# Weighted sums as 64-row, 32-column tiles in two of 32 units of an attention kernel

## The chip, the cores and the metric

The kernel runs on one core of a Trainium2 chip. The metric is the device time of one execution in microseconds (us). A core has five engines that work side by side: TensorE (PE, matrix products; its weight loads are listed apart as PEld), VectorE (DVE), ScalarE (ACT), GpSimd (POOL), and SyncE (SP), which here only issues DMAs. Each takes its instructions in the order in which the program lists them. TensorE's products land in PSUM banks of 128 partitions by 512 fp32 values; DVE and ACT read them there.

## What is computed

The reference mixes two attentions over the same 2048 positions of width 512, with 32 heads of 16 values each. Branch A looks back over 8 positions, 2 apart. Branch B is full attention with one shared key and value head. A gate per position mixes them.

```python
def _B_ref(x, wq, wk, wv, wo):
    q = (x @ wq).reshape(B, S, H, Dh).transpose(0, 2, 1, 3)
    k = x @ wk
    v = x @ wv
    scores = einsum("bhqd,bkd->bhqk", q, k) * (Dh ** -0.5)
    p = softmax(scores, axis=-1)
    o = einsum("bhqk,bkd->bhqd", p, v)
    return o.transpose(0, 2, 1, 3).reshape(B, S, H * Dh) @ wo

g = sigmoid((x * gate_w).sum(-1, keepdims=True))
return g * _A_ref(...) + (1 - g) * _B_ref(...)
```

The change concerns `o` of branch B: the sum over the keys of softmax weight times value.

## The kernel before

Branch B is cut into 32 **units**: 4 blocks of 512 queries by 8 groups of 4 heads. A unit takes 16 **steps**, one for each block of 128 keys, so the main loop (L1272) runs over 512 steps `s`, with `u, kt = divmod(s, 16)`.

A step does the following on its engines.

- `exp_pair` (L577), called twice: two score products on PE (L582), each of 64 rows (one half of the array for each of two heads), into the two halves of one double bank (`eb[0]` or `eb[1]`), and then one exponential on ACT over both (L584), which gives a tile `pexp`. A double bank is written again only after ACT has read it.
- `weighted` (L589), for the step before: the four heads' `pexp` tiles are multiplied with the block's values `vst`, which have 16 value columns and 16 columns of ones. The matmul of head `i` contracts all 128 keys and writes 32 partitions of the bank `po`. The four outputs together fill `po`, which gathers the sums over the unit's 16 steps. These are fp32 products, and each shows in the profile as two rows, while the scores are of a type that shows one row.
- Maxima for later units. The softmax needs each query's largest score before its unit begins, so the scores are formed once more with the queries as rows (L393) and reduced by DVE. `fill_pair` forms two into the double bank `m2` (named `pm` in the profile; reduced at L422), usually once a step. `fill_one` forms one, a **single**, into the bank `m1` (named `ps`; L433), where `singles` (L986) allows it.

After the last step of a unit, `finish_a` (L604) transposes `po` on DVE into `tt`. `finish_b` takes the reciprocal of the sums on DVE and scales on POOL. The next unit's weighted sums write `po` again, so they wait for the transpose.

The order of all instructions is fixed as the program is written out: a planner keeps a clock for each engine (`clk`) and a time at which each bank comes free (`free`), advanced by `after` with assumed durations, and decides by them what is issued where. `fill_ready` (L1011) issues a pair or a single only if its bank is expected to be free in time. `single_share` (L995) sets the rate of singles: the maxima still to go, less two for each step left (the pairs) and less an allowance for the output phases, divided by the steps left, at most one a step. `singles` spends that share. No single is asked for in a unit's first step until the last units.

Twice, at about 824 us and 1166 us, an output phase (`out_phase`, L864) stands between two units. It multiplies finished rows with the output weights and forms maxima beside them in another way (L491). Branch A's attention runs on POOL through the first two thirds of the span, and its projections on PE before the first unit.

Of the kernel before, what the change touches and what calls it, by code (L numbers as in the profile page):

```python
# [6 lines left out]
F32 = mybir.dt.float32  # L7
F32R = mybir.dt.float32r
AF = mybir.ActivationFunctionType
# [4 lines left out]
P = 128  # L14
# [4 lines left out]
NJ = S // P  # L19
# [26 lines left out]
M2H = 0.15  # L46
JUST = 0.05
WB = 6


T_R, T_LAT, T_EXP, T_RED2, T_RED1, T_W, T_TTR = 0.23, 0.20, 0.92, 1.14, 0.61, 1.21, 0.66
# [30 lines left out]
def gated_mix_kernel(ctx, tc, xt, wa, wk, wq, wo_a, wo_b, out):  # L82
    nc = tc.nc
# [11 lines left out]
    vst = cp.tile([P, NJ, 32], F32, name="vst")  # L95
# [14 lines left out]
    m1 = pp.tile([P, 512], F32, name="ps")  # L110
    po = pp.tile([P, 512], F32, name="po")
# [5 lines left out]
    def split(hi, lo, src, eng=None):  # L117
        high(hi, src)
        (eng or nc.vector).tensor_sub(lo, src, hi.bitcast(F32))

    clk = {"pe": 0.0, "act": 0.0, "dve": 0.0}

    def after(eng, ready, dur):
        clk[eng] = max(clk[eng], ready) + dur
        return clk[eng]
# [17 lines left out]
    raw = [first[:, k, :] for k in range(4)]  # L143
    raw += [p1.tile([P, 512], F32, name="xraw", tag=tag, bufs=WB) for tag in ("wah", "wal") for _ in range(6)]
    xraw = {(t, c): raw[C * t + c] for t in range(NQB) for c in range(C)}
# [15 lines left out]
    def load_wa(gg, c):  # L161
        waraw[gg, c] = p1.tile([P, GN], F32, name="waraw", bufs=2)
        nc.gpsimd.dma_start(waraw[gg, c], wa[c * P:(c + 1) * P, gg * GN:(gg + 1) * GN])

    def split_wa(gg, c):
        nonlocal pool
        wah[gg, c] = p1.tile([P, GN], F32R, name="wah", bufs=WB)
        wal[gg, c] = p1.tile([P, GN], F32R, name="wal", bufs=WB)
        split(wah[gg, c], wal[gg, c], waraw.pop((gg, c)), nc.gpsimd)
        after("act", clk["pe"], 0.62)  # L170
        pool = max(pool, clk["pe"] * 1e3) + 1300

    def ahead_wa(gg, k):

        if 0 <= k < 2 * C and k % 2 == 0:
            load_wa(gg, k // 2)
        if 2 < k <= (2 * C if gg == 0 else 2 * (WB - C)) + 1 and k % 2:
            split_wa(gg, (k - 3) // 2)
# [193 lines left out]
    free = {"m2": 0.0, "m1": 0.0, "e0": 0.0, "e1": 0.0, "po": 0.0}  # L372
# [22 lines left out]
    def to_go():  # L395
        return 2 * len(slots) + len(half)
# [178 lines left out]
    pe, pexp, exped = [], {}, {}  # L575
# [12 lines left out]

    def weighted(s):  # L589
        u, kt = divmod(s, NJ)  # L590
        for i in (3, 2, 1, 0):
            nc.tensor.matmul(po[32 * i:32 * i + 32, :], vst[:, kt, :], pexp[s, i // 2][:, i % 2, :], start=(kt == 0), stop=(kt == NJ - 1))  # L592
        del pexp[s, 0], pexp[s, 1]
        after("pe", exped.pop(s) + 0.1, T_W)

# [7 lines left out]

    def finish_a(u, eng):  # L604
        tt = pe[0].tile([P, 4 * 4, 32], F32, name="tt", bufs=2)
        nc.vector.transpose(tt.rearrange("p b d -> p (b d)"), po)
        at = after("dve", clk["pe"] + T_LAT, 0.7)
        tasks.append((clk["pe"] + 0.5, finish_b, (u, tt, eng)))

# [375 lines left out]

    def singles(s):  # L986

        most = to_go() - 2 * max(0, 16 * (NU - 1) - 16 - s) - PER_ROW * max(0, NJ - 4 - outs)
        need = -0.6 if s > NJ and s % NJ == 1 else 0.3 if bare[0] else 0.5 if (s + 1) % NJ == 0 else 1.0
        if most <= 0 or share[0] < need or not bare[0] and s % NJ != 1 and share[0] < 2.0 and clk["dve"] - clk["pe"] > BEHIND:  # L990
            return False
        share[0] -= 1.0
        return True
# [228 lines left out]
    def done_mm(at):  # L1222
        nonlocal pool
        x, i = at
        lump = lumps[x]
        if lump[0] == "a" and lump[2] == NJ - 1 and lump[1] + 1 < GG and i in (2, 5) and WB - C < 4:
            c = WB - C + (i == 5)
            if c < C:
# [43 lines left out]
    for s in range(NS + 1):  # L1272
        u, kt = divmod(s, NJ)
# [16 lines left out]
        rows = 4 if outs else 8  # L1290
# [23 lines left out]
        while order:  # L1314
            which = order.pop(0)
            if which == "later":
                order[:0] = ["m1", 1] if free["e1"] > clk["pe"] - E1S or bare[0] and free["m1"] < clk["pe"] - 1.0 else [1, "m1"]
                first = 0
            elif which == "m2":
                fill_ready("m2", M2S)  # L1320
            elif which == "m1":
                one = not later_rows and (kt or not s or u >= NU - 8) and singles(s)
                bare[0] = not one
                if one:
                    first = half[0][4] if half else 0
                    fill_ready("m1", M1S)
            elif s < NS:
                if which == 1:
                    spread_some(some)
                exp_pair(s, which % 2 or which // 2, which == 2, first)  # L1330
        if s == NS:
            spread_some(some)
        if s:
            weighted(s - 1)
            if kt == 0 and s < NS:
                finish_a(u - 1, nc.gpsimd)
# [14 lines left out]
    tt = pe[0].tile([P, 16, 32], F32, name="ttl", tag="tt", bufs=2)  # L1351
# [4 lines left out]
    both = pe[0].tile([P, 2, 256], F32, name="own2", tag="tt", bufs=2)  # L1356
# [61 lines left out]
```

## Time and profile before

| | us |
|---|---|
| median of 3 runs | 1452.81 (1452.70 to 1452.86) |
| span of the profiled execution (first to last instruction) | 1450.8 |
| PE busy | 1443.6 |
| ACT busy | 1284.9 |
| DVE busy | 1192.2 |
| POOL busy | 994.6 |

The profile page is from one execution, recorded by the hardware. It has each engine's busy time, and a chain of work that ended last: from the last instruction back, at each step, to what released it. Its views list instructions in groups (by line, engine and shape, with their count and mean length) or in order of time; in brackets stands the idle time of the engine ahead of an instruction and what ended it. "128*32 128x512" at a matmul means 128 rows and 32 columns of the array, and 128 x 512 values that stream through. Matmuls overlap, and their ends are modelled, so the distance from start to start says more than a length.

Most of the span is the 512 steps. Units 10 and 12 lie at about 590 to 624 us and 657 to 691 us, between the end of the front part (about 260 us) and the first output phase.

### The profile page before, as it was taken

To read this page: it belongs to the slowest core of one execution; us is meant where nothing else is said; L and a number is where in the kernel's file an instruction comes from. 1 tells how busy PE (TensorE), PEld (TensorE's weight loads), DVE (VectorE), ACT (ScalarE), POOL (GpSimd) and SP (SyncE) were. 2 spreads that over 40 slices of the span, in tenths; PEclk is the share of its full clock that TensorE was granted. 3 is DMA by queue.
4 is the path that set the end of the run, shared out by engine and by line. 5 is a ranking of instruction groups with operands and counts; after the bars stand their busy time and mean duration, and the time that the engine had idled before them with its cause. 6 is when DMAs were issued, how large, how long until landed. Compare 5 with 4: busy or idle time off the path is not lost.

```text
span 1450.8 us, 29082 instructions
## 1 busy us (share of the span) xinstructions
PE 1443.6 (100%) x10620; PEld 678.7 (47%) x10620; DVE 1192.2 (82%) x1867; ACT 1284.9 (89%) x1628; POOL 994.6 (69%) x1748
## 2 busy tenths in 40 slices
PE   9999999999999999999999999999999999999998
PEld 7977777433333333333333476333333364333343
DVE  8978889688888888888888888888888888888712
ACT  6659888999999999999999888999999988999986
POOL 7952989869898888888988899797888240011121
PEclk9999999999999999999999999999999999999999
DMA  7753433212021120211211202021120000000110
GB/s 238 221 157 103 125 104 97 64 57 87 14 85 42 46 90 13 72 42 42 83 42 42 72 24 98 12 72 42 42 72 12 12 27 16 13 2 1 29 32 29
DMA packets 75775, 89.80 MB, mean 62 GB/s; under 512 B 56880, under 2 KB 56928, under 8 KB 71408
## 3 DMA queue, kind: packets, MB, share of 16 engines
q1 hardware_dynamic: 68544, 48.74, 11.9%
q0 software_dynamic: 6368, 37.90, 7.8%
q8 instruction: 83, 1.36, 0.4%
q10 hardware_dynamic: 720, 1.31, 0.3%
q14 instruction: 60, 0.49, 0.1%
HBM read 60.03 MB, written 27.35 MB: 60 GB/s over the span
## 4 chain that ended last, share of the span: by engine, by line
PE 99%; DVE 1%; ACT 0%; issue 0%; POOL 0%; DVEq 0%; POOLq 0%; ACTq 0%
PE po L592 35%; PE pe L582 24%; PE pe L1219 12%; PE pm L393 8%; PE ps L393 6%; PE pe L876 4%; PE pm L491 3%; PE ps L491 2%; PE po L491 2%; PE pm L947 1%; PE pe L227 1%; PE po L193 0%; PE po L393 0%; PE pm L1219 0%; PE po L1046 0%
## 5 line engine op out<-in xcount | busy, mean ns | idle before, releaser
L584 ACT ACTIVATE pexp<-pe 128x1024 f32<-128x1024 f32 x1022 | 987.1, 1022 | 80.3 <-PE pe L582 76.8
L422 DVE TENSOR_REDUCE mx<-pm 128x2 f32<-128x1024 f32 x507 | 620.1, 1223 | 140.6 <-PE pm L393 136.8
L592 PE MATMUL po<-pexp,vst 128*32 128x512 f32 x4096 | 545.5, 605 | 0.0
L582 PE MATMUL pe<-qst,kst 64*128 64x512 f32 x1916 | 443.9, 451 | 0.0
L582 PEld LDWEIGHTS pe<-qst,kst 64*128 64x128 f32 x1916 | 179.9, 183 | 473.4 <-ACT pexp L584 466.2
L433 DVE TENSOR_REDUCE mx<-ps 128x1 f32<-128x512 f32 x400 | 272.1, 680 | 0.5 <-PE ps L393 0.5
L393 PE MATMUL pm<-kst,qst 62*128 62x512 f32 x978 | 198.1, 397 | 0.4 <-ACT pexp L584 0.4
L656 POOL TENSOR_TENSOR pr<-aext 128x256 f32<-128x256 f32 x256 | 182.1, 738 | 3.0 <-DMA aext<-ad 2.8
L716 POOL TENSOR_TENSOR oa<-oa,av 128x256 f32<-128x256 f32 x224 | 164.0, 732 | 15.1
L592 PEld LDWEIGHTS po<-pexp,vst 128*32 128x32 f32 x4096 | 80.5, 108 | 163.8 <-issue 155.1
L393 PE MATMUL ps<-kst,qst 62*128 62x512 f32 x392 | 154.3, 394 | 0.0
L713 POOL TENSOR_TENSOR av<-aext,lg 128x256 f32<-128x256 f32 x224 | 139.3, 622 | 13.3
L520 ACT ACTIVATE dd<-pm 128x512 f32<-128x512 f32 x180 | 101.5, 606 | 16.4 <-PE pm L491 8.0
L1219 PE MATMUL pe<-wah,xl 64*128 64x512 f32 x376 | 110.0, 394 | 0.0
L1219 PE MATMUL pe<-wal,xh 64*128 64x512 f32 x376 | 108.6, 394 | 0.0
L1219 PE MATMUL pe<-wah,xh 64*128 64x512 f32 x376 | 107.7, 395 | 0.4 <-DVE stage L324 0.3
L393 PEld LDWEIGHTS pm<-kst,qst 62*128 62x128 f32 x978 | 95.4, 186 | 3.6 <-ACT pexp L584 0.9
L662 POOL TENSOR_TENSOR tr<-pr 128x512 f32<-128x512 f32 x64 | 81.8, 1278 | 4.5
L520 ACT ACTIVATE pexp<-pm 128x512 f32<-128x512 f32 x124 | 70.1, 606 | 14.1 <-PE pm L491 7.0
L662 POOL TENSOR_TENSOR tr<-tr 128x256 f32<-128x256 f32 (+1 forms) x128 | 72.4, 566 | 8.5
L619 POOL TENSOR_TENSOR rl<-rl,gate_t 128x16 f32<-128x16 f32 x31 | 6.9, 222 | 103.0 <-DVE rl L613 95.3
L393 PEld LDWEIGHTS ps<-kst,qst 62*128 62x128 f32 x392 | 73.2, 187 | 3.7 <-issue 1.2
(226 smaller groups left out, 1993.9 us busy)
## 6 DMA issues: line engine op xcount, KB each, us to landing
aext<-ad POOLq DMA_DIRECT2D x32, 1056.0 KB, 5.5
qst<-qd SPq DMA_DIRECT2D x60, 128.0 KB
ad<-stage SPq DMA_DIRECT2D x32, 240.0 KB
qd<-qhi SPq DMA_DIRECT2D x16, 256.0 KB
qd<-qlo SPq DMA_DIRECT2D x16, 256.0 KB
xraw<-xt SPq DMA_DIRECT2D x15, 256.0 KB
qst<-qd SPq DMA_DIRECT2D x60, 64.0 KB
qst<-ml SPq DMA_DIRECT2D x216, 2.0 KB
```

The lines of the kernel that those rows point to most:

```text
L393: nc.tensor.matmul(dst, qst[home(v)[0]][b:b + 62, pr, t * P:(t + 1) * P], kst[b:b + 62, kc * 512:(kc + 1) * 512], start=True, stop=True)
L422: nc.vector.tensor_reduce(m[:, :, pr, t, kc], dst, AX.X, ALU.max)
L433: nc.vector.tensor_reduce(m[:, odd, pr, t, kc:kc + 1], dst, AX.X, ALU.max)
L520: nc.scalar.activation(d[:, odd], m2[:, odd, :], AF.Abs)
L582: nc.tensor.matmul(bank[:, odd, :], kst[b:b + 64, kt * P:(kt + 1) * P], qst[home(u)[0]][b:b + 64, pr, :], start=True, stop=True)
L584: nc.scalar.activation(e, bank, AF.Exp, scale=SCALE)
L592: nc.tensor.matmul(po[32 * i:32 * i + 32, :], vst[:, kt, :], pexp[s, i // 2][:, i % 2, :], start=(kt == 0), stop=(kt == NJ - 1))
L656: nc.gpsimd.tensor_mul(pr[:, k], q, e[:, o:o + NH, AC:2 * AC])
L662: nc.gpsimd.tensor_add(nx, cur[:, :, 0:n], cur[:, :, n:2 * n])
L713: nc.gpsimd.tensor_mul(av, e[:, o:o + NH, 2 * AC:].rearrange("p j (h d) -> p j h d", d=DH), lg[:, w].unsqueeze(3).to_broadcast([P, NH, AG, ...
L716: nc.gpsimd.tensor_add(ao, ao, av)
L1219: nc.tensor.matmul(front[2 if x == last else x % 2][0][:, b, :], l[h], r[h], start=(i == 0), stop=(i == 3 * C - 1))
```

## The change

In units 10 and 12 each product of the weighted sum is cut in two along the keys. Keys 0 to 63 of the block go into `po` as before, keys 64 to 127 into `m1`, the bank that singles use. So each step has eight matmuls of 64 rows and 32 columns in place of four of 128 rows and 32 columns. At the unit's end ACT copies `m1` to a tile `both` in SBUF, DVE adds `po` to it, and the transpose reads that tile in place of `po`. The planner's clocks are charged 0.62 us on ACT and 0.66 us on DVE for it. Since `m1` gathers sums for the whole unit, `singles` allows none in these two units, nor in the first step after each. All else, the assumed duration of a weighted sum (`T_W`) too, is unchanged.

```diff
+HALVED = (10, 12)

     def weighted(s):
         u, kt = divmod(s, NJ)
-        for i in (3, 2, 1, 0):
-            nc.tensor.matmul(po[32 * i:32 * i + 32, :], vst[:, kt, :], pexp[s, i // 2][:, i % 2, :], start=(kt == 0), stop=(kt == NJ - 1))
+        if u in HALVED:
+            for i in (3, 2, 1, 0):
+                for h, dst in enumerate((po, m1)):
+                    rows = slice(64 * h, 64 * h + 64)
+                    nc.tensor.matmul(dst[32 * i:32 * i + 32, :], vst[rows, kt, :], pexp[s, i // 2][rows, i % 2, :], start=(kt == 0), stop=(kt == NJ - 1))
+        else:
+            for i in (3, 2, 1, 0):
+                nc.tensor.matmul(po[32 * i:32 * i + 32, :], vst[:, kt, :], pexp[s, i // 2][:, i % 2, :], start=(kt == 0), stop=(kt == NJ - 1))
         del pexp[s, 0], pexp[s, 1]

     def finish_a(u, eng):
         tt = pe[0].tile([P, 4 * 4, 32], F32, name="tt", bufs=2)
-        nc.vector.transpose(tt.rearrange("p b d -> p (b d)"), po)
+        acc = po
+        if u in HALVED:
+            acc = pe[0].tile([P, 512], F32, name="both", bufs=1)
+            nc.scalar.activation(acc, m1, AF.Copy)
+            nc.vector.tensor_add(acc, po, acc)
+            free["m1"] = after("dve", after("act", clk["pe"] + T_LAT, 0.62), 0.66)
+        nc.vector.transpose(tt.rearrange("p b d -> p (b d)"), acc)

     def singles(s):
+        if s // NJ in HALVED or s % NJ == 0 and s // NJ - 1 in HALVED:
+            return False
```

## The prediction

> **What bounds the kernel now.** I read the page first: the busy shares, and the chain of work that ended last.
>
> ```profile
> span 1450.8 us, 29082 instructions
> PE 1443.6 (100%) x10620; PEld 678.7 (47%) x10620; DVE 1192.2 (82%) x1867; ACT 1284.9 (89%) x1628; POOL 994.6 (69%) x1748
> PE 99%; DVE 1%; ACT 0%; issue 0%; POOL 0%; DVEq 0%; POOLq 0%; ACTq 0%
> ```
>
> PE sets the end, with ACT close behind. These are averages, so I read the two changed units in the timeline. Here are two steps in unit 10 (a step is one round of the loop at L1272). The columns are start, length, engine and line.
>
> ```profile
> 619.35 1.06 PE L592 MATMUL po<-pexp,vst 128*32 128x512 f32 x8
> 620.35 0.50 PE L582 MATMUL pe<-qst,kst 64*128 64x512 f32 x2
> 620.68 0.40 PE L393 MATMUL pm<-kst,qst 62*128 62x512 f32 x2
> 620.92 0.40 PE L582 MATMUL pe<-qst,kst 64*128 64x512 f32 x2
> 621.16 0.39 PE L393 MATMUL ps<-kst,qst 62*128 62x512 f32 x1
> 621.47 0.16 PEld L592 LDWEIGHTS po<-pexp,vst 128*32 128x32 f32 x8 [0.36 <-issue]
> 621.47 1.06 PE L592 MATMUL po<-pexp,vst 128*32 128x512 f32 x8
> 623.38 1.06 PE L592 MATMUL po<-pexp,vst 128*32 128x512 f32 x8
> ```
>
> From one weighted sum to the next takes 2.12 us (619.35 to 621.47) when the step holds a single maximum product (`ps`), and 1.91 us (621.47 to 623.38) in the next step, which has none. **A single costs 0.21 us.** A step without one I call bare. Most bare steps stand alone. Where several follow each other, near the end of the maxima, it looks different:
>
> ```profile
> 1363.16 1.07 PE L592 MATMUL po<-pexp,vst 128*32 128x512 f32 x8
> 1364.75 3.84 ACT L584 ACTIVATE pexp<-pe 128x1024 f32<-128x1024 f32 x4 [0.18 <-PE pe L582]
> 1365.06 1.06 PE L592 MATMUL po<-pexp,vst 128*32 128x512 f32 x8
> 1366.74 0.19 PEld L582 LDWEIGHTS pe<-qst,kst 64*128 64x128 f32 x2 [0.35 <-ACT pexp L584]
> 1367.17 1.06 PE L592 MATMUL po<-pexp,vst 128*32 128x512 f32 x8
> 1368.17 0.49 PE L582 MATMUL pe<-qst,kst 64*128 64x512 f32 x2
> 1368.79 1.02 ACT L584 ACTIVATE pexp<-pe 128x1024 f32<-128x1024 f32 x1 [0.20 <-PE pe L582]
> 1369.08 0.64 PE L592 MATMUL po<-pexp,vst 128*32 128x512 f32 x4
> ```
>
> The steps are 1.90, 2.11 and 1.91 us: they alternate. A first bare step uses up ACT's slack. In the second, PE's scores wait for ACT to release the bank (0.35, at 1366.74); the weighted sum then keeps PE until 1368.17, so ACT in turn gets its input 0.20 late. **A run of bare steps costs 2.01 us each**, and ACT's own four exponentials (3.84) set a floor of 1.92.
>
> **The change, part by part.** First, `singles` returns False in units 10 and 12 and in the first step after each. I cut windows of 18 steps, from the weighted sum ahead of the unit's first bare step to that of the second step of the next unit; the rows are window, then DVE busy on L433 with the count of singles.
>
> ```profile
> 588.06:625.52 37.46, 9.53 (x14) 1.00 0.16 52
> 654.71:692.13 37.42, 8.86 (x13) 1.00 0.11 35
> 1098.42:1132.40 33.98, 9.45 (x14) 1.00 0.05 15
> 1337.15:1370.22 33.07, 7.55 (x12) 1.00 0.10 24
> ```
>
> All 18 steps become bare (the single of the second step also fails, since the planner holds `m1` until the add). 18 x 2.01 = 36.2, against 37.46 and 37.42: **-2.5 us** for both. At the floor, 18 x 1.92 = 34.6, it would be -5.7; at 2.11 each it would be +1.1. I take 2.01 because it is the row of exactly this case.
>
> Second, the weighted sums: 8 tiles of 64 rows and 32 columns in place of 4 of 128 rows. No row shows such a tile. The nearest are these, with those of the unit's end:
>
> ```profile
> L592 PE MATMUL po<-pexp,vst 128*32 128x512 f32 x4096 | 545.5, 605 | 0.0
> L592 PEld LDWEIGHTS po<-pexp,vst 128*32 128x32 f32 x4096 | 80.5, 108 | 163.8 <-issue 155.1 <-DVE tt L606 6.1 <-DVE mx L537 0.8
> L816 ACT ACTIVATE two<-pe 128x512 f32<-128x512 f32 x12 | 7.6, 632 | 0.9 <-PE pe L876 0.9
> L821 DVE TENSOR_TENSOR two<-pe,two 128x512 f32<-128x512 f32 x12 | 8.2, 686 | 0.0
> L606 DVE STREAM_TRANSPOSE tt<-po 128x512 f32<-128x512 f32 x31 | 22.1, 713 | 0.7
> ```
>
> Each source matmul shows as two rows of 605 ns, so eight rows a step, yet they take 1.06 together: two passes, the second 1.06 - 0.605 = 0.455 after the first, with the four column tiles side by side. The first four, cut at 1369.08, take 0.64, so tiles start about 0.01 apart (0.035 over three). The scores show the other direction: two 64-row products run side by side in 0.40 to 0.50, into two banks. I assume that both go together and eight tiles share a pass: four more starts, +0.04 a weighted sum. In the alternating run a weighted sum lies on the path once in two steps, so 32 x 0.02 = **+0.6**. The bounds: four tiles at a time, +0.91 each (two more passes); or all waits around it gone, -0.3 each (rivals below). I take the near end: all eight outputs lie apart.
>
> The Trainium skill, "TensorE: Matmul & The Clock Gate", Measured speedup vs the span model, has packed tiles cost one matmul's duration plus about 4 ns a tile; by that four more tiles are an estimated +0.02, and the sum moves by 0.3.
>
> Third, the unit's end. Before, the transpose frees `po`:
>
> ```profile
> 623.10 3.82 ACT L584 ACTIVATE pexp<-pe 128x1024 f32<-128x1024 f32 x4 [0.21 <-PE pe L582]
> 624.51 0.72 DVE L606 STREAM_TRANSPOSE tt<-po 128x512 f32<-128x512 f32 x1
> 625.28 1.17 DVE L422 TENSOR_REDUCE mx<-pm 128x2 f32<-128x1024 f32 x1
> 625.52 1.07 PE L592 MATMUL po<-pexp,vst 128*32 128x512 f32 x8
> ```
>
> After, ACT must first copy `m1`. Its queue holds the step's two exponentials, done near 625.0 (half of 3.82). The copy (0.63) ends at 625.6, the add (0.69) at 626.3, and only then may PE start the next unit's weighted sum: 626.37 in place of 625.52, **+0.85 twice, +1.7**. Behind that sum on PE wait the next scores, and for them ACT. ACT's next exponentials are themselves 0.6 late. On DVE the transpose (0.71, now from SBUF) and the next pair's reduction (1.17) wait behind the add; the planner sees the pair bank late and skips one pair a unit, which takes 0.24 off PE (620.68 to 620.92): **-0.5** for two. POOL gets the reciprocal about 1.5 us later, twice; in unit 10 it has 5 us to spare:
>
> ```profile
> 588.06:625.52 37.46, 37.46 (x268) 13.65 (x267) 33.12 (x42) 34.89 (x38) 32.48 (x68) 1.00 0.16 52
> ```
>
> (window, then PE, PEld, DVE, ACT and POOL busy: POOL 32.48 of 37.46; the clock is granted in full). SP gets nothing new. Bounds: +0.4 each (only the copy, less ACT's 0.20 slack) to +2.0 (the pair not skipped, so PE waits for its reduction as well).
>
> Fourth, and largest: the maxima not formed must be formed elsewhere. `single_share` recomputes the rate from what is left, so they come back as singles, spread over the bare steps of later units. They are 14 + 13 singles, and two pairs, which is 4 more: 31 x 0.21 = **+6.5**. No other work covers them: each lengthens a PE step. Bounds: 0, if they all slip in beside other work; 0.45 each by units with 12 and 14 (33.07 and 33.98), which differ in more than singles, +14.
>
> Sum: -2.5 + 0.6 + 1.7 - 0.5 + 6.5 = **+5.8 us**. The profiled span of 1450.8 becomes 1456.6. The median of the runs, 1452.81, stands 2.0 above the span; with that, **1458.6 us**.
>
> **The rivals.** *The tiles take turns.* If only four run at a time, a weighted sum takes 0.91 more, and PE alone then bounds the step: 1.91 + 0.91 = 2.82. 32 x (2.82 - 2.01) = +25.9, less the 0.6: 1484. For it: no row shows row and column tiles together. Against: each works alone. 12%.
>
> *The switch costs nothing any more, and it ends not slower.* Now PEld idles 0.36 ahead of L592's loads and the scores behind need 0.50 in place of 0.40: products of 64 rows give way to ones of 128. If the wait comes from the row count, 64 rows throughout would let loads go ahead: about 0.3 off each weighted sum. ACT then binds at 1.92, so only 32 x 0.09 = 2.9 is gained, and the 0.6 falls away: 1458.6 - 3.5 = 1455.1, within 0.2%. It decides only if the wait follows rows rather than the whole tile shape. 16%.
>
> The Trainium skill, "TensorEngine Tiling (Array Packing)", Key Properties, says that changing the tiling mode drains the engine; by it 64x128 to 64x32 is still a change and this rival gives nothing. The 0.36 agrees that a change of shape waits, but cannot say which dimension matters.
>
> *The displaced maxima are free.* If the two output phases, where PE products of other shapes run beside them, took all 31: 1458.6 - 6.5 = 1452.1, no change. Against: how many those phases fill depends on bank times, not on what is left. 7%. With the rival before it, 1448.6, faster: 3%.
>
> **How the numbers follow.** The forecast, 1458.6, has 62%; its own range is 1456 to 1466 (the bounds of the unit's end and of the price of a single, less likely at the far end). I reach down to 1451.8, for the free maxima, and up to 1467; left out are the tiles in turns (12%) and the fastest case (3%). 0.2% is 2.9 us, about what a measurement of this kernel can tell from no change. Faster by that: 3%. Within: 16 + 7 and 1 of the forecast's lower tail, 24%. Slower: 61 + 12, 73%.
>
> **What would show it.** L592 in the two units: 16 rows a step within about 1.1 us, or about 2. The steps in units 10 and 12: alternating near 1.9 and 2.1, or all at 1.92 with PEld's 0.36 gone. At each unit's end a wait of PEld on the add near 0.8. L433: none in the units, near 14 a unit afterwards, the same number in all, give or take the pairs. The forecast fails most if the tiles take turns, or if the later units are no longer than before.

## The result, and the profile after

| | before | after |
|---|---|---|
| median of the runs, us | 1452.81 | 1460.83 (1460.57 to 1460.95, 3 runs) |
| span of the profiled execution, us | 1450.8 | 1459.2 |

The ratio is 1.0055, with a 95% interval of 1.0035 to 1.0075: 8.0 us slower, against a forecast of 5.8. The page of the kernel after has these lines on busy time, the chain that ended last, and three of the costliest groups.

```profile
span 1459.2 us, 29574 instructions
PE 1448.4 (99%) x10876; PEld 676.4 (46%) x10876; DVE 1197.6 (82%) x1866; ACT 1283.0 (88%) x1622; POOL 994.6 (68%) x1748
...
PE 96%; DVE 1%; ACT 1%; DMA 0%; POOL 0%; issue 0%; ACTq 0%; DVEq 0%
...
L423 DVE TENSOR_REDUCE mx<-pm 128x2 f32<-128x1024 f32 x510 | 623.8, 1223 | 145.8 <-PE pm L394 143.2
L599 PE MATMUL po<-pexp,vst 128*32 128x512 f32 x3840 | 511.4, 605 | 1.8 <-DVE both L617 1.4
...
L434 DVE TENSOR_REDUCE mx<-ps 128x1 f32<-128x512 f32 x409 | 278.3, 680 | 0.5 <-PE ps L394 0.5
```

PE still sets the end. Its lines have moved: the normal weighted sums are at L599, the halved ones at L596, the scores at L583, maxima at L394, pair and single reductions at L423 and L434. New waits are small here: 1.4 us of PE on the add (L617). The last row counts 9 more singles than before (400), and L423 3 more pairs (507), though the maxima of the whole kernel are the same. That is read further down.

**The tiles.** These are the groups of the halved sums, by shape, and then a weighted sum of unit 10 in the timeline (start, length, engine, line; in brackets the idle time ahead).

```profile
L596 PE MATMUL po<-pexp,vst 64*32 64x512 f32 x256 | 34.6, 601 | 0.0
L596 PE MATMUL ps<-pexp,vst 64*32 64x512 f32 x256 | 34.6, 601 | 0.0
L596 PEld LDWEIGHTS po<-pexp,vst 64*32 64x32 f32 x256 | 5.6, 104 | 7.8 <-issue 7.3 <-DVE tt L619 0.5
```

```profile
598.19 0.10 PEld L596 LDWEIGHTS po<-pexp,vst 64*32 64x32 f32 x1 [0.24 <-issue]
598.19 0.61 PE L596 MATMUL po<-pexp,vst 64*32 64x512 f32 x1
598.20 0.61 PE L596 MATMUL ps<-pexp,vst 64*32 64x512 f32 x1
...
598.24 0.61 PE L596 MATMUL ps<-pexp,vst 64*32 64x512 f32 x1
598.64 0.59 PE L596 MATMUL po<-pexp,vst 64*32 64x512 f32 x1
...
599.21 0.19 PEld L583 LDWEIGHTS pe<-qst,kst 64*128 64x128 f32 x2 [0.84 <-ACT pexp L585]
...
600.32 0.10 PEld L596 LDWEIGHTS po<-pexp,vst 64*32 64x32 f32 x1 [0.25 <-issue]
...
602.24 0.10 PEld L596 LDWEIGHTS po<-pexp,vst 64*32 64x32 f32 x1 [0.25 <-issue]
```

All eight tiles start within 0.05 us and run side by side; the second pass follows 0.45 after the first. From the first tile to the next scores it takes 1.02 (598.19 to 599.21), against 1.00 before (619.35 to 620.35). The steps are 2.13 and 1.92: they alternate, as the bare runs of before did. All 32 halved sums show the same 1.02. And the wait ahead of the loads is still there, 7.8 us over 32 weighted sums, 0.24 each.

**The unit's end.** Here is that of unit 10, where ACT copies, DVE adds and transposes, and PE waits.

```profile
623.99 0.60 ACT L616 ACTIVATE both<-ps 128x512 f32<-128x512 f32 x1
...
624.63 0.69 DVE L617 TENSOR_TENSOR both<-po,both 128x512 f32<-128x512 f32 x1 [1.09 <-ACT both L616]
625.35 0.71 DVE L619 STREAM_TRANSPOSE tt<-both 128x512 f32<-128x512 f32 x1
625.37 0.16 PEld L599 LDWEIGHTS po<-pexp,vst 128*32 128x32 f32 x8 [1.03 <-DVE both L617]
...
626.98 2.86 ACT L585 ACTIVATE pexp<-pe 128x1024 f32<-128x1024 f32 x3 [0.55 <-PE pe L583]
627.03 0.16 PEld L599 LDWEIGHTS po<-pexp,vst 128*32 128x32 f32 x8 [0.36 <-issue]
```

The chain is the one predicted: exponentials, copy, add, PE. The unit's last step, from the weighted sum at 622.45 to the one at 625.37, takes 2.92, some 0.8 over an ordinary one (2.84 at the end of unit 12); ACT's next exponentials are 0.55 late. The step behind it takes 1.66, since it has neither a pair nor a single. Units 10 and 12 take 33.14 and 33.13 us from first weighted sum to first weighted sum, against 33.36 and 33.38 before. So the changed units themselves became 0.2 us **shorter**. The loss lies elsewhere:

| stretch (units) | after minus before, us | singles more |
|---|---|---|
| 10 to 12 | -0.4 | -26 |
| 13 | +1.0 | 0 |
| 14, 15 | +1.2 | 4 |
| 16, with the first output phase | -3.2 | 1 |
| 17 to 23 | +3.8 | 13 |
| 24, with the second output phase | +0.9 | 3 |
| 25 to 29 | +3.2 | 15 |
| 30, 31, to the last weighted sum | +1.8 | 0, but 9 maxima in unit 30's pair bank |

The rows add up to 8.3; the two profiled spans differ by 8.4.

**The later units** hold more singles. The first fence has unit windows of the kernel before, the second the same units after: window, length, then DVE busy on the reductions of singles with their count.

```profile
998.98:1032.43 33.45, 8.85 (x13) 1.00 0.22 72
1304.36:1337.91 33.55, 8.84 (x13) 1.00 0.01 2
```

```profile
999.45:1033.33 33.88, 10.21 (x15) 1.00 0.24 77
1309.37:1343.62 34.25, 10.89 (x16) 1.00 0.00 1
```

Two more singles cost 0.43 us, three 0.70: 0.21 and 0.23 each. These are two units out of many. By the table, units 14, 15, 17 to 23 and 25 to 29 together are 8.2 us longer with 32 more singles, 0.26 each.

The later units hold 36 more singles, and besides them a pair in unit 16 and 9 maxima in unit 30: 47 maxima more. The change displaced 31, as many as forecast: 27 singles (one stands just ahead of unit 10's first weighted sum, so the table has 26) and the pair skipped at each of the two unit ends. The other 16 come from the output phases, which form fewer maxima than before. The first fence is the group of their products into the pair bank in the kernel before, the second after.

```profile
L491 PE MATMUL pm<-q,qst 62*128 62x512 f32 x124 | 48.2, 402 | 0.0
```

```profile
L492 PE MATMUL pm<-q,qst 62*128 62x512 f32 x116 | 44.6, 401 | 0.0
```

The other two banks fell from 62 to 58 each: 16 maxima left the phases for the steps, all of them from the first phase. Unit 16, which holds it, is 3.2 shorter, but each maximum then costs a step its 0.2. The phase's length does not follow the count alone: in two kernels further down 8 maxima fewer in that phase go with a unit 16 that is 3.0 shorter (the change with the displaced maxima left out) and 0.5 shorter (the first nudged kernel). What else sets it was not traced.

**Unit 13** holds just as many singles as before and is 1.0 longer. One step, from 698.00 to 701.05, makes the difference:

```profile
698.00 0.16 PEld L599 LDWEIGHTS po<-pexp,vst 128*32 128x32 f32 x8 [0.37 <-issue]
...
698.40 0.22 POOL L713 TENSOR_TENSOR asum<-half 128x16 f32<-128x16 f32 x1
...
698.65 0.25 DVE L703 RECIPROCAL asum<-asum 128x16 f32<-128x16 f32 x1 [1.51 <-POOL asum L713]
698.82 1.16 DVE L423 TENSOR_REDUCE mx<-pm 128x2 f32<-128x1024 f32 x1
...
700.04 0.19 PEld L394 LDWEIGHTS pm<-kst,qst 62*128 62x128 f32 x2 [0.85 <-DVE mx L423]
...
701.05 0.16 PEld L599 LDWEIGHTS po<-pexp,vst 128*32 128x32 f32 x8 [0.25 <-issue]
```

POOL's sum for branch A is late. DVE's reciprocal waits 1.51 for it, the pair's reduction waits behind the reciprocal in DVE's queue, and PE waits for the pair bank. POOL itself had waited before that, at the end of unit 12:

```profile
691.00 0.69 DVE L617 TENSOR_TENSOR both<-po,both 128x512 f32<-128x512 f32 x1 [1.08 <-ACT both L616]
...
692.37 0.33 DVE L690 TENSOR_REDUCE amx<-lg 128x16 f32<-128x128 f32 x1
...
692.77 0.46 POOL L695 TENSOR_TENSOR lg<-lg,amx 128x128 f32<-128x128 f32 x1 [4.63 <-DVE amx L690]
```

POOL waited 4.63 for a maximum of branch A (L690), which stands in DVE's queue behind the change's add and the transpose, and the add had waited 1.08 for ACT's copy. The kernel before has no such wait of POOL there.

### The profile page after: what moved, and what is told of

It is laid out like the page before. It is cut to its first block, busy times and chain, and to the rows that moved or that the text cites. A ratio compares the mean times of both kernels' runs of the same rounds, so it can differ in the third digit from the quotient of the medians.

```text
span 1459.2 us, 29574 instructions
## 1 busy us (share of the span) xinstructions
PE 1448.4 (99%) x10876; PEld 676.4 (46%) x10876; DVE 1197.6 (82%) x1866; ACT 1283.0 (88%) x1622; POOL 994.6 (68%) x1748
## 4 chain that ended last, share of the span: by engine, by line
PE 96%; DVE 1%; ACT 1%; DMA 0%; POOL 0%; issue 0%; ACTq 0%; DVEq 0%
PE po L599 32%; PE pe L583 23%; PE pe L1234 12%; PE pm L394 8%; PE ps L394 6%; PE pe L889 4%; PE pm L492 3%; PE po L596 2%; PE ps L492 1%; PE po L492 1%; PE pm L960 1%; ACT pexp L585 1%; PE pe L228 1%; DMA wqr<-wq 0%; DVE mx L423 0%
## 5 line engine op out<-in xcount | busy, mean ns | idle before, releaser
L423 DVE TENSOR_REDUCE mx<-pm 128x2 f32<-128x1024 f32 x510 | 623.8, 1223 | 145.8 <-PE pm L394 143.2
L599 PE MATMUL po<-pexp,vst 128*32 128x512 f32 x3840 | 511.4, 605 | 1.8 <-DVE both L617 1.4
L583 PE MATMUL pe<-qst,kst 64*128 64x512 f32 x1916 | 441.0, 451 | 0.1
L583 PEld LDWEIGHTS pe<-qst,kst 64*128 64x128 f32 x1916 | 180.2, 183 | 476.5 <-ACT pexp L585 468.0
L434 DVE TENSOR_REDUCE mx<-ps 128x1 f32<-128x512 f32 x409 | 278.3, 680 | 0.5 <-PE ps L394 0.5
L394 PE MATMUL pm<-kst,qst 62*128 62x512 f32 x985 | 199.3, 396 | 1.3 <-ACT pexp L585 0.8
L394 PE MATMUL ps<-kst,qst 62*128 62x512 f32 x401 | 159.0, 397 | 0.0
L599 PEld LDWEIGHTS po<-pexp,vst 128*32 128x32 f32 x3840 | 75.5, 108 | 161.3 <-issue 150.9
L394 PEld LDWEIGHTS pm<-kst,qst 62*128 62x128 f32 x985 | 95.7, 187 | 4.4 <-ACT pexp L585 1.4
L521 ACT ACTIVATE pexp<-pm 128x512 f32<-128x512 f32 x116 | 65.9, 607 | 13.5 <-PE pm L492 9.5
L394 PEld LDWEIGHTS ps<-kst,qst 62*128 62x128 f32 x401 | 74.9, 187 | 5.7 <-DVE mx L434 1.9
```

The source lines that it names most:

```text
L394: nc.tensor.matmul(dst, qst[home(v)[0]][b:b + 62, pr, t * P:(t + 1) * P], kst[b:b + 62, kc * 512:(kc + 1) * 512], start=True, stop=True)
L423: nc.vector.tensor_reduce(m[:, :, pr, t, kc], dst, AX.X, ALU.max)
L434: nc.vector.tensor_reduce(m[:, odd, pr, t, kc:kc + 1], dst, AX.X, ALU.max)
L521: nc.scalar.activation(d[:, odd], m2[:, odd, :], AF.Abs)
L583: nc.tensor.matmul(bank[:, odd, :], kst[b:b + 64, kt * P:(kt + 1) * P], qst[home(u)[0]][b:b + 64, pr, :], start=True, stop=True)
```

## The experiments

Theory A: the displaced maxima carry the loss. Theory B: the tiles and units' ends do. Later came C, that a change in the order of later work costs time by itself, and D, which joins A and C. "Before" in each comparison is the kernel before on the same chip.

### The ban alone, and the ban with the displaced maxima left out

The first kernel has the ban on singles and nothing else. The second leaves the 26 displaced maxima out altogether, products and reductions.

```diff
+HALVED = (10, 12)
     def singles(s):
+        if s // NJ in HALVED or s % NJ == 0 and s // NJ - 1 in HALVED:
+            return False
```

> The kernel before with nothing but the ban on singles in units 10 and 12 (and the first step after each); the weighted sums stay 128 rows deep, nothing is copied. Theory A, the displaced maxima carry the cost: the 8.0 us of the change less its two unit ends (0.8 each) and the eight-tile passes (0.3), so about 1459 us. Theory B, the tiles and the unit's end carry it: the two units lose 2.5 us and little comes back, 1450 to 1454 us. In the profile both expect steps of 1.90 and 2.11 us by turns in units 10 and 12.

Measured: 1457.46 us, ratio 1.0034 (1.0021 to 1.0047), +5.0. That is 1.5 below A's value and 3.5 above B's range. Units 10 and 12 take 32.15 and 32.27.

```diff
         share[0] -= 1.0
+        if s // NJ in HALVED or s % NJ == 0 and s // NJ - 1 in HALVED:
+            leave_one()
+            return False
         return True
+
+    def leave_one():
+        if not half:
+            v, pr, t, kc = slots.pop(0)
+            half.extend([(v, pr, t, kc, 0), (v, pr, t, kc, 1)])
+        v = half.pop(0)[0]
+        unit_tile(v)
+        filled(v, 1)
```

> As the one before, but the maxima that the ban displaces are left out: they are counted as formed, with no product and no reduction (26 maxima are missing from the result's inputs), so that the later units have as much to do as before. Theory of the run of bare steps, 2.01 us each: 1452.8 - 2.5 = 1450.3 us. Rival, ACT's floor of 1.92 a step: about 1447 us. Rival, every bare step at 1.90 as when it stands alone: about 1446 us.

Measured: 1452.19 us, ratio 0.9997 (0.9987 to 1.0006), -0.2. The two kernels differ by 5.3 us over 26 maxima, 0.20 each, and their output phases form equally many. That is A's price. But the second missed its expectation: it was 2.5 us ahead at unit 14, as expected, and lost nearly all of it behind that, though it has no more maxima to form there than the kernel before (8 of them are formed in steps instead of in the output phases). These windows are units 10 and 12 of the kernel with the ban alone; window, length, then DVE busy on singles (none).

```profile
592.24:624.39 32.15, 0.00 (x0) 1.00 0.15 48
657.73:690.00 32.27, 0.00 (x0) 1.00 0.16 47
```

Against 33.14 after, the tiles and the unit's end cost about 0.9 a unit. Twice that and the 1.0 of unit 13 come to 2.8; the change and the ban alone differ by 3.0.

### The change with the displaced maxima left out, and in one unit only

The first has the change, with `leave_one` in place of the ban (27 maxima left out). The second has the whole change in unit 10 alone.

```diff
-HALVED = (10, 12)
+HALVED = (10,)
```

> The changed kernel, with the displaced maxima left out in the same way (27 maxima are not formed; the two pairs skipped at the unit ends still come back). Theory A: 1450.3 for the run of bare steps, + 1.7 for the unit ends, + 0.3 for the passes of eight, + 0.8 for the pairs, so about 1453 us. Theory B: the cost stays, 1458 to 1461 us.

Measured: 1454.79 us, ratio 1.0016 (1.0007 to 1.0026), +2.4. So 5.6 of the 8.0 us go with the maxima; unit 13 takes 33.14 here, so about 1.0 of it is the stall there, and 4.6 over 27 is 0.17 each. B fell, but A's 1453 was 1.8 too low; the excess is taken up where the order is held fixed.

> The change in unit 10 alone. Theory A, each unit displaces its own maxima at the same price: half of the 8.0, about 1456.8 us. Rival, the cost grows with the backlog (the stall of 0.9 us in unit 13 of the changed kernel, the later start of the last rows): less than half, 1454 to 1455.5 us.

Measured: 1456.81 us, ratio 1.0030 (1.0018 to 1.0042), +4.4, about half of the change's 8.0 and just A's value. The parts are not all halves: 16 maxima are displaced (14 singles and a pair), but only 4 leave the output phases, and there is no step like the one of 3.05 in unit 13. So the exact match is in part luck.

### The copy on DVE

ACT's copy waits behind two exponentials; DVE is idle at that time.

```diff
-            nc.scalar.activation(acc, m1, AF.Copy)
+            nc.vector.tensor_copy(acc, m1)
```

> The changed kernel with one instruction moved: DVE, not ACT, copies the second bank at the two unit ends; the planner's charges stay, so every other instruction keeps its place. Theory: the wait of PE at a unit's end is the copy's place in ACT's queue (it started 1.54 us after the last weighted sum's start, where DVE was idle from about 1.1 on) plus its 0.6 and the add's 0.7. DVE starts the copy about 0.4 earlier, so the boundary step falls from 2.9 to about 2.5 us and the time by 0.7 to 0.9 us. Rival: what DVE has to do next (the transpose, the pair's reduction) starts no earlier and holds PE as before: no change.

Measured: 1460.56 us, ratio 1.0056 (1.0041 to 1.0071): no difference from the change that the intervals can tell. Its timeline at the end of unit 10:

```profile
623.29 0.69 DVE L616 COPY both<-ps 128x512 f32<-128x512 f32 x1
...
624.01 0.69 DVE L617 TENSOR_TENSOR both<-po,both 128x512 f32<-128x512 f32 x1
...
624.76 0.16 PEld L599 LDWEIGHTS po<-pexp,vst 128*32 128x32 f32 x8 [0.81 <-DVE both L617]
...
626.36 1.94 ACT L585 ACTIVATE pexp<-pe 128x1024 f32<-128x1024 f32 x2 [0.70 <-PE pe L583]
```

PE's wait falls from 1.03 to 0.81 and units 10 and 12 to 32.91 and 32.98, a gain of 0.4 us in the two together. The expected 0.7 to 0.9 was too much: the unit's last step takes 2.67 in place of 2.92. The copy starts 1.20 after the start of the last weighted sum in place of 1.54, and takes 0.69 on DVE against 0.60 on ACT. Where the 0.4 went by the end was not settled; several later units are 0.2 longer.

### One reciprocal later

One reciprocal of branch A (L703, in unit 13) is put four DVE instructions later; nothing else moves.

```diff
-                hooks.append((pool + 800, a_sum, g, ("sum", g, hf)))
+                hooks.append((pool + (3300 if 676 < clk["pe"] < 690 else 800), a_sum, g, ("sum", g, hf)))
```

> The changed kernel with one DVE reciprocal of branch A (the one that waited 1.51 us for POOL at 698.65) placed four DVE instructions later; the order of all other instructions is unchanged. Theory, the step of 3.05 us in unit 13 comes from that wait on DVE, which makes the pair's reduction and then PE late: the step falls to about 2.13 and the time by 0.9 us. Rival, PE is late there for a reason of its own: no change.

Measured: 1459.51 us, ratio 1.0048 (1.0033 to 1.0063), 1.05 below the kernel with the copy on DVE in the same comparison and 1.3 below the change's median. The timeline of unit 13 now runs:

```profile
697.19 1.23 DVE L423 TENSOR_REDUCE mx<-pm 128x2 f32<-128x1024 f32 x1 [0.53 <-PE pm L394]
...
697.93 0.22 POOL L713 TENSOR_TENSOR asum<-half 128x16 f32<-128x16 f32 x1
...
699.69 0.16 PEld L599 LDWEIGHTS po<-pexp,vst 128*32 128x32 f32 x8 [0.37 <-issue]
```

POOL's sum comes as late as before against the weighted sum (0.38 behind the one at 697.55, 0.40 behind 698.00), but the pair's reduction no longer stands behind it. The step is 2.14 in place of 3.05, and unit 13 falls from 34.40 to 33.54. The stall was POOL, through DVE's queue, to PE.

### The kernel before with its planner nudged

The planner's POOL clock alone is moved once, at step 224. The maxima to be formed are the same; what changes is the order from unit 14 on, and with it where each is formed.

```diff
     for s in range(NS + 1):
+        if s == 224:
+            charge(4500.0)
```

> The kernel before, with no work added, taken away or reshaped: only the planner's estimate of POOL is set 4.5 us later once, at the start of unit 14, so that the later instructions fall in another order (the output phases then form fewer maxima, the steps more). Theory C, the 2.3 us that the kernels without the displaced maxima lost after unit 16 come from such a reshuffling: 1 to 3.5 us longer than the kernel before. Rival, the order does not matter: within 0.4 us of it.

> The same with 1.0 us in place of 4.5. Theory C: 0.5 to 1.5 us longer than the kernel before. Rival: within 0.4 us of it.

The second has 1000.0 in place of 4500.0. Measured: 1454.14 us, ratio 1.0011 (1.0001 to 1.0020), and 1454.15, ratio 1.0010 (1.0000 to 1.0020): +1.3 each, as theory C has it, though the second interval reaches down to no change. The groups of the first nudged kernel show what moved:

```profile
L433 DVE TENSOR_REDUCE mx<-ps 128x1 f32<-128x512 f32 x414 | 281.7, 680 | 0.5 <-PE ps L393 0.5
...
L491 PE MATMUL pm<-q,qst 62*128 62x512 f32 x116 | 45.2, 401 | 0.0
```

Its output phases form 16 maxima fewer, exactly as many as in the changed kernel (116 where before has 124, and 4 fewer in each of the other two banks), and 14 come back as singles. Nothing was displaced here. The equal 1.3 arise in different places. In the first nudged kernel units 16 and 24, which hold the phases, are 1.2 us shorter together, and units 25 to 29, with 12 of those singles, 2.9 longer. In the second the phases form 12 fewer, and unit 24 alone is 1.4 longer. So a changed order costs time here, but not through one mechanism, and not so much for each maximum that moves.

### The order held fixed

This settles what the missed expectation left open. The 25 singles of both units are left out, but the planner is charged as if they had been formed, so that all other instructions keep their places.

```diff
+        if not muted[0]:
             max_mm(dst, v, pr, t, kc, odd)
             nc.vector.tensor_reduce(m[:, odd, pr, t, kc:kc + 1], dst, AX.X, ALU.max)
...
+                    muted[0] = s // NJ in HALVED or s % NJ == 0 and s // NJ - 1 in HALVED
                     fill_ready("m1", M1S)
+                    muted[0] = False
```

> The kernel before with the singles of units 10 and 12, and of the first step after each, left out (product and reduction), while the planner's clocks are charged as if they had been formed: every other instruction keeps its place. Theory D (changing the later order by itself cost some 2 us in the run that left the displaced maxima out): the 2.3 us that the bare steps of both units gain stay to the end, 1452.8 - 2.3 = 1450.5 us. Rival (whatever is gained there is lost again later, in any order, as that run ended only 0.2 below the kernel before): 1452.3 to 1452.8 us.

Measured: 1450.50 us, ratio 0.9985 (0.9976 to 0.9994), -2.1. Theory D gave 1450.5. Its output phases form as many as before:

```profile
L494 PE MATMUL pm<-q,qst 62*128 62x512 f32 x124 | 48.4, 403 | 0.0
```

So a bare unit does gain, and the 1.9 us that the earlier run (26 left out) lost are the price of a changed order.

The second kernel adds the tiles, the copy and the add of the change (its `weighted` and `finish_a`, without the charge to the clocks).

> The same, with the 64-row tiles, the copy and the add of the change in units 10 and 12, none of them charged to the planner, so that the order stays that of the kernel before. Theory D: 1450.5 + 0.2 twice for the tiles + 0.8 twice for the units' ends = 1452.5 us, up to 0.5 more since no pair is skipped; if POOL's lateness stalls unit 13 here as well, 1453.5. Rival (the order costs nothing; the tiles and ends themselves cost more than their steps show): 1454.8 us, the time of the change without its displaced maxima. Units 10 and 12 near 33.2 us each by both.

Measured: 1454.38 us, ratio 1.0011 (1.0003 to 1.0020), +1.8. That lies between the values of D and the rival, so it missed both; units 10 and 12, at 33.13 each, are as both had it. Its timeline and the step after unit 10 say why:

```profile
624.17 0.69 DVE L619 TENSOR_TENSOR both<-po,both 128x512 f32<-128x512 f32 x1 [1.08 <-ACT both L618]
...
624.92 0.16 PEld L601 LDWEIGHTS po<-pexp,vst 128*32 128x32 f32 x8 [0.43 <-DVE both L619]
...
626.88 0.18 PEld L394 LDWEIGHTS pm<-kst,qst 62*128 62x128 f32 x2 [0.78 <-DVE mx L423]
...
627.55 0.16 PEld L601 LDWEIGHTS po<-pexp,vst 128*32 128x32 f32 x8 [0.37 <-issue]
```

No pair is skipped, because the planner is not told. So the pair's product waits 0.78 for the reduction, which waits behind add and transpose; the step takes 2.63 (624.92 to 627.55), and units 11 and 13 take 34.15 and 34.14 in place of 33.2 and 33.4. With 0.86 in units 10 and 12 each, an uncharged end costs 1.7. The planner's charge is therefore worth some 0.8 a unit: it skips the pair that would wait.

### More singles in full units

To price a single by itself, the kernel before forms products a second time in bare steps of units 17 to 22.

```diff
                 bare[0] = not one
+                if not one and kt and 17 <= u <= 22 and dup[0]:
+                    dup[0] -= 1
+                    max_mm(m1, u, 0, 0, 0, 0)
+                    void = wp.tile([P, 1], F32, name="void", bufs=2)
+                    nc.vector.tensor_reduce(void, m1, AX.X, ALU.max)
```

> The kernel before with 26 more singles in the bare steps of units 17 to 22 (products formed a second time, their reduced values unused), not charged to the planner, so nothing else moves. Theory D with the price of the prediction: 26 x 0.21 = 5.5, 1458.3 us. Rival (the 0.20 that the earlier pair of runs gave for a displaced maximum was partly the cost of a changed order; the bare price is about half): 1455.5 us.

Measured: 1456.65 us, ratio 1.0028 (1.0017 to 1.0039), +4.1. The expectation counted wrongly: only 11 bare steps were left there, not 26. So the price is 0.37 each, above both theories. The view of the added line says what is in it (who waited for it, us and times), and the timeline shows one such wait:

```profile
PEld ps L393: 3.1, 10
```

```profile
923.19 0.68 DVE L1328 TENSOR_REDUCE void<-ps 128x1 f32<-128x512 f32 x1
...
923.93 0.18 PEld L393 LDWEIGHTS ps<-kst,qst 62*128 62x128 f32 x1 [0.56 <-DVE void L1328]
```

An unplanned single still holds `m1` when the next planned one needs it. Some 3.1 us of waits by the weight loads are not 3.1 us of time, as part is hidden, but they cover the 0.16 each above the plain price. The run gives an upper bound, no price.

## Why the prediction was right, point by point

- **Eight tiles share a pass.** Right; 0.02 a weighted sum was measured where 0.04 was taken. The rival in which tiles take turns fell. Tiles start 0.007 apart (0.05 over seven gaps). The Trainium skill, "TensorE: Matmul & The Clock Gate", Measured speedup vs the span model, has about 4 ns a tile; the trace here has 7 ns, and the trace decides.
- **The switch.** The wait ahead of the loads stayed, 0.24 a weighted sum (7.8 over 32), so this rival fell too. The Trainium skill, "TensorEngine Tiling (Array Packing)", Key Properties, has any change of tiling mode drain the engine; by that rule, which the trace agrees with at 0.24 to 0.25 though it does not show what the wait is for, 64x128 to 64x32 is still a change.
- **Bare steps at 2.01.** Right as a mechanism: alternating 1.92 and 2.13. With the order kept, two bare units gave 2.1 us, against 2.5 forecast.
- **The unit's end.** +0.85 forecast, 0.7 to 0.8 measured, by the predicted chain; the wait on the add was 1.03, where near 0.8 was expected. Skipping a pair did not return 0.24: the next step is that much longer (2.38). It avoided a wait, as the run with the uncharged end showed. Tiles and ends come to about 0.87 a unit (33.14 against 32.27 with the order kept), 1.7 for two; the terms gave 1.8.
- **Displaced maxima at 0.21.** The price was right: 0.20 (the ban with and without them) and 0.17 (the change with and without them). The count was right too: 31 were displaced. Of these 26 or 27 were left out in the runs, which is 4.6 to 5.3 us; with the two pairs, at 0.17 to 0.20, 31 make 5.3 to 6.2, and the forecast had 6.5. "The same number in all, give or take the pairs" failed for L433: 9 more, for the reason that follows.
- **What the sum lacked.** First, the step "POOL gets the reciprocal about 1.5 us later, twice; in unit 10 it has 5 us to spare" failed at the end of unit 12. What held POOL up was not the reciprocal but branch A's maximum, placed behind the add in DVE's queue (4.63), and POOL's busy share of a unit says nothing on who waits for it next. It cost 0.9 to 1.0. Second, the prediction said that what the output phases fill depends on bank times, and took their number as fixed. The planner's times moved, and 16 maxima left the phases. A reordering alone cost 1.3 us in the two nudged kernels and 1.9 in the run of the ban without the displaced maxima.

Together: -2.1 + 1.7 + 1.0 + 5.3 + 1.9 = 7.8, against 8.0 measured. The terms come from different kernels and are not strictly additive; the split between displaced maxima and order is good to perhaps 1 us. The change without its 27 singles gives a second value for the order: of its 2.4 us, -2.1 + 1.7 and 0.8 for the two pairs that come back are explained, which leaves 2.0. The forecast lay only 2.2 below the measured time partly by luck: it left out 2.9, and its own terms were 0.9 too high against this sum. Why the phases of the changed orders fill fewer was read off as a count, not traced to one bank, and why a changed order is slower was not traced to one cause. No version that forms all maxima is faster than the kernel before: with the displaced maxima formed, the tiles have nothing to pay for them, since a weighted sum takes as long as it did.

## What to carry to other kernels

Before an accumulator is put into a bank, price the work that the bank held, and where that work goes: here this was most of the loss, while the tiles themselves were nearly free. When a planner writes out the order, part of a measured difference is that of the reshuffled order; hold the order fixed, charging the clocks for what is left out, before a part is given a price. An engine with slack can still stall the one that sets the end, if a third engine's queue stands between them.

## What the runs showed of the hardware that was not expected

Tiles of 64 rows and 32 columns, four column groups by two row halves in two PSUM banks, all ran at once: eight fp32 products in 1.02 us, as long as four of 128 rows took (1.00), with loads of 104 ns against 108. The wait ahead of the loads, where score products stand just before them, was the same whether the rows changed (64x128 to 128x32, 0.25 at 623.38 in the kernel before) or not (64x128 to 64x32, 0.24 to 0.25).
